# Chunked attention, then an ELU feed-forward network: exchanging 32x32 blocks of the turned probabilities by ScalarE copies in place of four transfers

## The chip, the core and the metric

The kernel runs on one core of a Trainium2 chip. The metric is the device time of the whole program in microseconds (us); less is better. "Before" is the kernel as it stood, "after" the changed one. The engines are named as the profile names them: PE (TensorE), PEld (its weight loads), DVE (VectorE), ACT (ScalarE), POOL (GpSimd), and SP (SyncE), which here issues every transfer.

## The reference

Softmax attention inside chunks of 64 tokens, then a feed-forward network on the 4608 rows of 512 features that it gives. q, k and v are 8 x 8 x 576 x 64 (batch, heads, tokens, head size), all in float32.

```
scores = q_c @ k_c.T / sqrt(64)            # per batch, head and chunk of 64 tokens
a      = exp(scores - max) / (sum + 1e-9)
x      = (a @ v_c)                         # back to 4608 x 512
h      = x @ w_in                          # 512 -> 2048
out    = elu(h) @ w_out                    # 2048 -> 512
```

## The kernel before

**The work.** The 4608 tokens are 9 blocks of 512 (`NB`), each of 4 tiles of 128 tokens (`NTT`); a tile holds two chunks of 64 tokens. The feed-forward part needs products in full float32, which are made from three products of a high and a low part (`three`, L434: `a_hi b_hi + a_hi b_lo + a_lo b_hi`). Blocks 0 to 2 do it plainly: for each of 16 slices `f` of the hidden features, 12 matmuls make `h` (`hidden`), ACT does relu and exp (L468, L469), DVE combines them to the elu (L471), ACT casts the high part (L476), DVE or POOL makes the low part (L479), and 12 matmuls add the slice to the output (`second_products`). The later blocks are taken in pairs as one 2 x 2 block product with seven products in place of eight (Strassen's scheme): one pair by code written out by hand (`Pair`, L725, then `KEPT`), the last two pairs of blocks from a planner (`Plan`, L820; there the exp is taken head by head, L1515).

**The attention of a tile** runs inside the feed-forward work of an earlier block, a step at a time. For tiles 8 to 35 (class `Later`) the steps are: load q and k (`load_qk`), transpose them on DVE in blocks of 32 x 32 (`turn`, L351), 32 score matmuls (`score`, L248), subtract the maximum (L361, L362), exp on ACT (L367), the sums on DVE (L372 to L374), then `turn_a`: multiply by the inverse sums (L380), transpose the probabilities on DVE (`turn_out`, L388) into `turned`, copy that to `unturned` on ACT (`copy_turned`, L393) and exchange blocks (`swap_turned`, L399). DVE's transpose turns each 32 x 32 block where it stands, so for a 64 x 64 chunk the two off-diagonal blocks still lie in each other's group of 32 partitions. `swap_turned` puts them right with four transfers of 32 x 256 floats (32 KB each): two chunks (`c`) times two blocks (`e`). Last come 32 matmuls with v (`times_v`, L256), which read `turned`, and a copy of the result (`keep_x`, L420).

**What sets the order.** Every engine carries out its instructions in the order in which the program gives them. In the third block that is a string for each `f` (`EVEN`, `ODD`, `THIRD_BLOCK`): `H` is `hidden(f)`, each `e` the next step of the elu, `P` the 12 output matmuls; `h` is `turn_a`, `q` and `k` the transposes, `s` the scores, `v` and `x` the product with v and its copy, `l` and `V` loads, `w` a step that prepares sums of w_out on POOL, ACT and DVE (L576 to L597). A tile takes two slices: `h` at the end of the odd slice or the start of the even one, `q` and `k` in the even one, `s` and `v` in the next odd one. In the pairs the items are `p1` to `p7` (a product of 6 matmuls), `c` (ACT copies it out, L758), `d` (DVE adds it up, L762), `1` to `4` (elu steps), `Q` (3 output matmuls) and the attention's letters. `SUMS_AT` says behind which items a `w` step goes. In the planner each job has engines with costs and keys that it reads and writes; a list scheduler gives each engine the ready job that is due first, where due times come from PE's sequence. The order that comes out is fixed when the program is built.

**Transfers** all go through SP's queue. A transfer is issued when SP reaches it, and each issue waits on one of eight transfer semaphores in turn, that is for the transfer eight places ahead of it; `swap_turned` waits besides for ACT's copy.

Of the kernel before, what the change touches and what calls it, by code (L numbers as in the profile page):

```python
# [20 lines left out]
def kernel(  # L21
# [19 lines left out]
    nc = tc.nc  # L41

    B, H, S, D = q.shape
# [4 lines left out]
    P = 128  # L48
    C = 64
# [6 lines left out]
    Q = 32  # L56
    PLAIN = 3
    NS = (NB - PLAIN) // 2
    NG = NF // 2
# [19 lines left out]
    turned, unturned = [const.tile([P, 2, H, Q], F32, name=name) for name in ("turned", "unturned")]  # L79
# [29 lines left out]
    def in_order(w):  # L109

        return w.rearrange("p (c b d) -> p b c d", b=4, d=Q)
# [218 lines left out]
    class Later:  # L330
# [42 lines left out]
            nc.vector.tensor_scalar_add(z_ps, z_ps, 1e-9)  # L373
            nc.vector.reciprocal(self.z, z_ps)  # L374

        def turn_a(self):

            nc.vector.tensor_tensor(  # L380
                out=self.scores, in0=self.scores, in1=self.z.broadcast_to([P, 2, NK, C]),
                op=ALU.mult)
            self.turn_out()
            self.copy_turned()
            self.swap_turned()
# [9 lines left out]
        def swap_turned(self):  # L395
            for c in range(2):
                for e in range(2):
                    to, of = [slice(c * C + i * Q, c * C + (i + 1) * Q) for i in (e, 1 - e)]
                    nc.sync.dma_start(out=turned[to, 1 - e], in_=unturned[of, e])  # L399

        def times_v(self):
            self.x_ps = banks[0][:, :, NK * C:].rearrange("p c (h t) -> p c h t", h=NK)
# [562 lines left out]
    def dma(n: int, took: float):  # L965
        return 540 * n, 540 * (n - 1) + 2000 + took, took

    class Tokens:
# [3 lines left out]
            self.now, self.following, self.after, self.done = now, following, None, set()  # L972

        def step(self, item: str):
            on = self.now if item in "mEzhvx" else self.following
            item = {"M": "m", "F": "E"}.get(item, item)
            if item == "l":
                if on and on.n + 1 < NB * NTT and not self.after:
                    self.after = Later(on.n + 1)
                    self.after.load_qk()  # L980
                return
            if not on or (on.n, item) in self.done:
                return
            self.done.add((on.n, item))
            {"m": on.less_max, "E": on.exp, "z": on.sums, "h": on.turn_a,
             "v": on.times_v, "x": on.keep, "q": lambda: on.turn(0), "k": lambda: on.turn(1),
             "s": on.score, "V": on.load_v}[item]()
            if item == "x":
                self.now, self.following, self.after = self.following, self.after, None

    def warm(n: int):
# [35 lines left out]

    EVEN, ODD = "l H e q e k e e P", "H s v e x V m E e e z h e P"  # L1030
    THIRD_BLOCK = {
# [16 lines left out]
    }  # L1048
    FIRST_PAIR = (
# [1 line left out]
        "3 3"  # L1051
    )
    SECOND_PAIR = (
        "p1 c1 5 5 h Q 4 p2 d1 4 Q q k p6 c2 1 Q Q 1 p5 1 1 Q l p7 c3 d2 Q Q 2 p4 c4 2 Q 3 p3 d3 "
        "3 3 3 s v x V"
    )
    PAIR = (
        "m p1 c1 4 E Q 4 z p2 d1 Q p6 c2 h 1 Q Q 1 p5 1 q k 1 Q l p7 c3 d2 Q Q 2 p4 c4 2 Q 3 p3 d3 "
        "3 3 3 s v x V"
    )  # L1060
    KEPT = (
# [16 lines left out]
    )  # L1078
    SUMS_AT = ("p1", "p2", "c2", "d2", "p4", "p3")

    ctx.enter_context(tc.manual_schedule(engines={
        mybir.EngineType.PE, mybir.EngineType.Activation, mybir.EngineType.DVE,
# [7 lines left out]
    with (  # L1090
# [19 lines left out]
        for item in START.split():  # L1110
            kind, n = item[0], item[1:]
# [61 lines left out]
    kept_st, unstored, banks, later, t3_place = [], [], [], {}, []  # L1173

    run, f, early_tiles = (0, o_tiles(), None), -1, {}
    for item in FIRST_BLOCK.split():
# [3 lines left out]
        elif item == "e":  # L1180
            g, acted = next(act), acted + 1
# [30 lines left out]
    for f in range(NF):  # L1212
        tt, st = divmod(f, 4)
        n = 2 * NTT + tt + 1
# [9 lines left out]
        for item in (LAST if f == NF - 1 else (LATER if tt else SECOND_BLOCK)[st]).split():  # L1224
            if item == "H":
                act, acted = elu(hidden(f)), 0
            elif item == "e":
                g, acted = next(act), acted + 1
# [21 lines left out]
    n = PLAIN * NTT  # L1250
# [61 lines left out]
    for f in range(NF):  # L1312
        for item in THIRD_BLOCK.get(f, ODD if f % 2 else EVEN).split():
            if item == "H":
                h = hidden(f)
                act, acted = elu(h, nc.gpsimd if 1 < f < NF - 1 else nc.vector), 0
            elif item == "e":
                g, acted = next(act), acted + 1
# [39 lines left out]
    for g in range(NG):  # L1358
        before, pair = pair, Pair(g)
        for item in ((FIRST_PAIR, SECOND_PAIR)[g] if g < 2 else PAIR).split():  # L1360
            if item[0] == "p":
                pair.product(int(item[1]))
            elif item[0] == "c":
                pair.keep(int(item[1]))
            elif item[0] == "d":
                pair.add(int(item[1]))
            elif item in "45":
                if before:
                    next(before.parts["3" if item == "5" else item], None)
            elif item in "123":  # L1370
                next(pair.parts[item])
            else:
                do(item)
            if item in SUMS_AT[4 if g == 0 else 0:4 if g == NG // 2 else 6] and g <= NG // 2:
                do("w")
    preparing, halves_kept, o_last = True, iter(range(NF)), o_tiles()
    run = n0 + TB, o_last, b_half_place
# [23 lines left out]
    plan = Plan()  # L1401
# [80 lines left out]
    def add_softmax(t: float, n: int, begun: bool = False):  # L1482
        mx = {}

        def in_bank(at: int = 0):
            at += NK * C
            return later[n].bank[:, :, at:at + NK].rearrange("p j (h e) -> p j h e", e=1)

        def maximum():
            mx[0] = in_bank(NK)  # L1490
            nc.vector.tensor_reduce(out=mx[0], in_=later[n].scores, axis=AX.X, op=ALU.max)

        def less():
            nc.vector.tensor_tensor(
                out=later[n].scores, in0=later[n].scores,
                in1=mx[0].broadcast_to([P, 2, NK, C]), op=ALU.subtract)

        def bias():
            mx[1] = sm.tile([P, 2, NK, 1], F32, name="mx")
            nc.vector.tensor_scalar_mul(mx[1], mx[0], -SCALE)  # L1500

        def normal():
            nc.vector.tensor_tensor(
                out=later[n].scores, in0=later[n].scores,
                in1=later[n].z.broadcast_to([P, 2, NK, C]), op=ALU.mult)

        plan.add(t + 1.0, "DVE", DVE_OP, maximum, ["psa"], [("mx", n), "xps"])
        if BY_HEADS and not begun:
            plan.add(t + 1.3, "DVE", (150, 172), bias, [], [("mx", n)])

            def exp_by_head():
                later[n].z = sm.tile([P, 2, NK, 1], F32, name="z")
                for j in range(2):
                    for h in range(NK):
                        nc.scalar.activation(  # L1515
                            out=later[n].scores[:, j, h, :], in_=later[n].scores[:, j, h, :],
                            func=AF.Exp, scale=SCALE, bias=mx[1][:, j, h, :],
                            accum_out=later[n].z[:, j, h, :])

                nc.scalar.activation(  # L1520
                    out=in_bank(), in_=later[n].z, func=AF.Copy, scale=1.0, bias=1e-9)

            def inverse():
                nc.vector.reciprocal(later[n].z, in_bank())
            plan.add(t + 2.0, "ACT", (2100, 2300), exp_by_head, [("mx", n)], ["psa"])
            plan.add(t + 2.5, "DVE", (190, 207), inverse, [], ["psa"])
        else:
            plan.add(t + 1.5, "DVE", DVE_OP, less, [], ["psa"])
            plan.add(t + 2.0, "ACT", ACT_PSUM, lambda: later[n].exp(), [], ["psa"])
            plan.add(t + 2.5, "DVE", (1000, 1110), lambda: later[n].sums(), [], ["psa"])  # L1530
        plan.add(t + 3.2, "DVE", DVE_OP, normal, [], ["psa"])
        plan.add(t + 3.7, "DVE", (630, 716), lambda: later[n].turn_out(), ["psa"], ["turned"])
        plan.add(t + 4.2, "ACT", ACT_OP, lambda: later[n].copy_turned(), ["turned"], ["unturned"])
        plan.add(t + 4.7, "SP", dma(4, 420), lambda: later[n].swap_turned(), ["unturned"], ["turned"])

    def add_turns(t: float, n: int):
        for i, to in enumerate(("qT", "kT")):
# [216 lines left out]
    for when, (job, f, tt, hi, lo) in zip([T0 - 1 + .05 * i for i in range(4)] + [T0 - .5 + .05 * i for i in range(4)],  # L1754
# [10 lines left out]
        if last:  # L1765
            place = g_first[:, 3, tt]
            e = "DVE" if tt % 2 else "ACT"
# [3 lines left out]
                             out=place.rearrange("p (b c d) -> p b c d", b=4, d=Q),  # L1771
                             in_=in_order(o_last[tt])),
# [3 lines left out]
                         out=out[n0 + TB + tt * P:n0 + TB + (tt + 1) * P, :], in_=place),  # L1776
# [59 lines left out]
```

## Time and profile before

| | |
|---|---|
| three timed runs | 839.7, 840.29 (median), 842.94 us |
| the profiled execution | 841.87 us, of which the span of the core's instructions is 840.1 us |
| PE busy in the span | 812.3 us (97%), 5853 matmuls |
| DVE, ACT, POOL busy | 620.0 us (74%), 525.0 us (62%), 172.8 us (21%) |
| transfers | 191.38 MB, mean 228 GB/s; 112 of them are `turned<-unturned` |
| mean granted PE clock | 0.991 of full speed |

The changed code runs in these stretches of the span, by the profile's own times: the third block from about 222 to 326 us, the pairs written by hand to 463, `KEPT` to 513, the first planned pair of blocks to about 700 us. Behind that no attention is left.

In a row of a list of groups stand line, engine and operation, out<-in by the program's names, sizes and count, and behind the bar the busy time in us, the mean of one in ns, and the engine's idle time just before with what ended most of it. In a row of the waits stand the waiting engine with its tile and line, what it waited for, and the total in us, the count and the longest. In a row of the timeline stand start in us, duration in us, engine, line and operation, and in brackets the idle time before it. PEclk is the clock granted to PE as a share of full speed.

### The profile page before, as it was taken

The numbers are of one execution on the slowest core, as the hardware profiler recorded it, in microseconds if no ns is written. First come the engines' busy times: TensorE is split into PE (matmuls) and PEld (weight loads), VectorE is DVE, ScalarE is ACT, GpSimd is POOL, SyncE is SP. The second block draws the span as 40 slices with busy tenths as digits, with TensorE's granted clock in tenths as the row PEclk, the third lists the DMA queues.
The fourth block names the chain that finished last, engine by engine and source line by source line (L and its number), as shares of the span: only waits on it lengthen the run. The fifth ranks groups of instructions, "written<-read, shape, count | busy, mean of one in ns | idle before, by whom it ended". The sixth has DMA issues, their size and how long they took to land.

```text
span 840.1 us, 15832 instructions
## 1 busy us (share of the span) xinstructions
PE 812.3 (97%) x5853; PEld 661.7 (79%) x5853; DVE 620.0 (74%) x908; ACT 525.0 (62%) x990; POOL 172.8 (21%) x147
## 2 busy tenths in 40 slices
PE   7899999999999989989999999999999999999996
PEld 6788888888778868868778888777888878888885
DVE  5999997666865748776756777867789956557954
ACT  5999876445544535755556544888967737776451
POOL 0000014365433411554211351000020000000101
PEclk9999999999999989999999999999999999999999
DMA  9974855889878986689997888998766585555654
GB/s 246 257 248 167 260 167 162 258 258 270 241 207 236 253 225 175 197 233 256 292 272 206 260 228 267 314 276 260 236 209 215 183 246 204 197 188 192 225 193 133
DMA packets 188653, 191.38 MB, mean 228 GB/s; under 512 B 82592, under 2 KB 157856, under 8 KB 188576
## 3 DMA queue, kind: packets, MB, share of 16 engines
q1 hardware_dynamic: 188576, 190.37, 75.7%
q8 instruction: 46, 0.75, 0.4%
q14 instruction: 31, 0.25, 0.1%
HBM read 143.65 MB, written 42.99 MB: 222 GB/s over the span
## 4 chain that ended last, share of the span: by engine, by line
PE 74%; DMA 12%; DVE 5%; SPq 4%; ACT 3%; issue 1%; DVEq 0%; ACTq 0%
PE o L434 41%; PE h L434 28%; DMA ring<-a_dram 2%; DMA turned<-unturned 2%; PE ps_a L256 2%; PE ps_a L248 2%; SPq L206 1%; DMA kept<-in_q_dram 1%; DMA v_sb<-in_v_dram 1%; DMA a_dram<-wi_hi 1%; DMA w_dram<-kept 1%; DMA st<-in_moe_w_out_dram 1%; DVE kept L542 1%; DMA w_dram<-g_kept 1%; SPq L227 1%
## 5 line engine op out<-in xcount | busy, mean ns | idle before, releaser
L434 PE MATMUL o<-wo_hi,ghi 128*128 128x512 f32 x272 | 108.7, 400 | 0.0
L434 PE MATMUL o<-wo_hi,glo 128*128 128x512 f32 x272 | 107.0, 394 | 0.2 <-DVE glo L479 0.2
L434 PE MATMUL o<-wo_lo,ghi 128*128 128x512 f32 x272 | 107.0, 393 | 0.0
L434 PE MATMUL h<-xhi,wi_hi 128*128 128x512 f32 x228 | 83.9, 396 | 0.0
L434 PE MATMUL h<-xlo,wi_hi 128*128 128x512 f32 x228 | 82.4, 390 | 0.5 <-DMA wi_hi<-a_dram 0.5
L434 PE MATMUL h<-xhi,wi_lo 128*128 128x512 f32 x180 | 70.2, 390 | 0.0
L434 PEld LDWEIGHTS o<-wo_hi,glo 128*128 128x128 f32 x272 | 51.6, 190 | 12.0 <-DVE glo L479 1.1
L434 PEld LDWEIGHTS o<-wo_hi,ghi 128*128 128x128 f32 x272 | 51.7, 190 | 11.4
L434 PEld LDWEIGHTS o<-wo_lo,ghi 128*128 128x128 f32 x272 | 51.7, 190 | 10.4
L510 POOL TENSOR_TENSOR kept<-wi_hi,wi_lo 128x512 f32<-128x512 f32 x16 | 24.8, 1566 | 156.1 <-DMA kept<-in_k_dram 116.4
L471 DVE SCALAR_TENSOR_TENSOR e<-e,h 128x512 f32<-128x512 f32 x48 | 32.8, 683 | 25.6 <-ACT e L469 25.6
L434 PE MATMUL o<-split,ring 128*128 128x512 f32 x216 | 50.9, 390 | 0.0
L434 PEld LDWEIGHTS h<-xhi,wi_hi 128*128 128x128 f32 x228 | 42.6, 188 | 9.7 <-ACT kept L758 0.6
L434 PEld LDWEIGHTS h<-xlo,wi_hi 128*128 128x128 f32 x228 | 42.7, 188 | 9.3 <-issue 0.9
L434 PEld LDWEIGHTS o<-split,ring 128*128 128x128 f32 x216 | 40.5, 188 | 8.4
L393 ACT COPY unturned<-turned 128x512 f32<-128x512 f32 x28 | 17.4, 620 | 45.4 <-DVE turned L388 45.4
L468 ACT ACTIVATE e<-h 128x512 f32<-128x512 f32 x48 | 28.8, 599 | 26.8 <-PE h L434 24.1
L476 ACT CAST ghi<-e 128x512 fp32r<-128x512 f32 x48 | 29.8, 621 | 19.5 <-DVE e L471 19.4
L434 PE MATMUL h<-split,ring 128*128 128x512 f32 x168 | 40.3, 391 | 0.0
L1441 ACT ACTIVATE e<-e 128x512 f32<-128x512 f32 x64 | 39.4, 630 | 1.1
L434 PEld LDWEIGHTS h<-xhi,wi_lo 128*128 128x128 f32 x180 | 33.8, 188 | 7.1
L361 DVE TENSOR_REDUCE mx<-ps_a 128x8 f32<-128x512 f32 x21 | 14.4, 688 | 32.0 <-ACT xf L420 31.4
(215 smaller groups left out, 2030.1 us busy)
## 6 DMA issues: line engine op xcount, KB each, us to landing
ring<-a_dram SPq DMA_DIRECT2D x56, 512.0 KB, 4.6
ring<-w_dram SPq DMA_DIRECT2D x56, 512.0 KB, 3.2
wi_hi<-a_dram SPq DMA_DIRECT2D x56, 256.0 KB, 5.9
kept<-in_q_dram SPq DMA_DIRECT2D x100, 128.0 KB, 3.0
kept<-in_k_dram SPq DMA_DIRECT2D x100, 128.0 KB, 3.7
wo_lo<-lo_dram SPq DMA_DIRECT2D x20, 512.0 KB, 6.2
v_sb<-in_v_dram SPq DMA_DIRECT2D x32, 256.0 KB, 5.1
st<-in_moe_w_in_dram SPq DMA_DIRECT2D x16, 512.0 KB, 4.3
```

Of the source, the lines that this page charges most:

```text
L206: nc.sync.dma_start(out=dst[p0:p0 + n], in_=src[b, :, s0:s0 + n, :].rearrange("h s d -> s h d"))
L227: nc.sync.dma_start(out=qk[p0:p0 + n // U, w0:w0 + NK * U * D].rearrange("p (h w) -> p h w", h=NK), in_=src[b, j::2, s0:s0 + n, :].rearran ...
L248: nc.tensor.matmul(scores[halves[c], j, hp, :], lhsT=qT[halves[j], hp, halves[c]], rhs=kT[halves[j], hp, halves[c]], start=True, stop=True,)
L256: nc.tensor.matmul(x_ps[halves[j], c, hp, :], lhsT=v_sb[halves[c], 2 * hp + j, :], rhs=aT[halves[c], :, j * NK + hp], start=True, stop=True,)
L361: nc.vector.tensor_reduce(out=mx, in_=self.scores, axis=AX.X, op=ALU.max)
L393: nc.scalar.copy(out=unturned, in_=turned)
L434: nc.tensor.matmul(ps, lhsT=a, rhs=b, start=start, stop=stop, skip_group_check=onto)
L468: nc.scalar.activation(out=e, in_=h, func=AF.Relu, scale=-1.0)
L471: nc.vector.scalar_tensor_tensor(out=e, in0=e, scalar=-1.0, in1=h, op0=ALU.add, op1=ALU.max)
L476: nc.scalar.copy(out=ghi, in_=e)
L510: nc.gpsimd.tensor_tensor(out=out, in0=a, in1=b, op=op)
L1441: nc.scalar.activation(out=units[u], in_=units[u], func=AF.Exp, scale=-1.0)
```

## The change

From the third block on, for 24 of the 28 tiles, `swap_turned` with its four transfers is not called; four ACT copies of 32 partitions x 256 floats, from one group of partitions to the other, write the same blocks. They come in two halves, one for each chunk (`swap_next`). In the third block both halves (`y y`) stand directly behind `H` of the even slice, and so ahead of that slice's relu and exp. In the pairs they stand behind `c3` and `c4`. In the planner each half is an ACT job of its own. `SUMS_AT` is moved so that one `w` step of the first pair falls in the second. The tiles of the second block keep the four transfers.

```diff
+        def turn_and_copy(self):
+            self.normalize()
+            self.turn_out()
+            self.copy_turned()
+            self.chunks = iter(range(2))
+
+        def swap_next(self):
+            c = next(self.chunks, None)
+            if c is not None:
+                for e in range(2):
+                    to, of = [slice(c * C + i * Q, c * C + (i + 1) * Q) for i in (e, 1 - e)]
+                    nc.scalar.copy(out=turned[to, 1 - e], in_=unturned[of, e])
...
-            {"m": on.less_max, "E": on.exp, "z": on.sums, "h": on.turn_a,
+            {"m": on.less_max, "E": on.exp, "z": on.sums, "h": on.turn_and_copy,
...
-    EVEN, ODD = "l H e q e k e e P", "H s v e x V m E e e z h e P"
+    EVEN, ODD = "l H y y e q e k e e P", "H s v e x V m E e e z h e P"
...
-        "m p1 c1 4 E Q 4 z p2 d1 Q p6 c2 h 1 Q Q 1 p5 1 q k 1 Q l p7 c3 d2 Q Q 2 p4 c4 2 Q 3 p3 d3 "
+        "m p1 c1 4 E Q 4 z p2 d1 Q p6 c2 h 1 Q Q 1 p5 1 q k 1 Q l p7 c3 y d2 Q Q 2 p4 c4 2 y Q 3 p3 d3 "
...
-        plan.add(t + 4.7, "SP", dma(4, 420), lambda: later[n].swap_turned(), ["unturned"], ["turned"])
+        for c in range(2):
+            plan.add(t + 4.7 + .1 * c, "ACT", (650, 850), swap(c), ["unturned"], ["turned", ("half", c)])
```

PE's order is the same in both kernels, instruction for instruction. What moves is shown at three places.

ACT's order in the third block, at the tile whose `h` is followed by a `w` step that casts `io`. First as before: `unturned<-turned` is `copy_turned`, `e<-h` and `e<-e` are relu and exp of the even slice.

```order
L393 COPY unturned<-turned 128x512
L588 CAST io<-io 128x1024
L468 ACTIVATE e<-h 128x512
L469 ACTIVATE e<-e 128x512
L476 CAST ghi<-e 128x512
```

The same place in the changed kernel:

```order
L393 COPY unturned<-turned 128x512
L601 CAST io<-io 128x1024
L412 COPY turned<-unturned 32x256 x4
L481 ACTIVATE e<-h 128x512
L482 ACTIVATE e<-e 128x512
```

The four copies stand between the attention's copy and the relu and exp of the slice; nothing else has moved there.

ACT's order in a pair of the hand-written part, from the copy of product 3 (`kept<-h`) to the elu of the second hidden slice (`e<-spare`), before:

```order
L758 COPY kept<-h 128x512
L708 ACTIVATE e<-g_kept 128x512
L709 ACTIVATE e<-e 128x512
L758 COPY spare<-h 128x512
L708 ACTIVATE e<-spare 128x512
```

And in the changed kernel:

```order
L771 COPY kept<-h 128x512
L412 COPY turned<-unturned 32x256 x2
L721 ACTIVATE e<-g_kept 128x512
L722 ACTIVATE e<-e 128x512
L771 COPY spare<-h 128x512
L412 COPY turned<-unturned 32x256 x2
L721 ACTIVATE e<-spare 128x512
```

Two copies stand ahead of each of the two elus.

SP's order in the third block, from a load of v on, before; `kept` is the place of the next q and k:

```order
L206 DMA v_sb<-in_v_dram 128x8x64
L399 DMA turned<-unturned 32x256 x4
L227 DMA kept<-in_q_dram 32x4x256 x4
L227 DMA kept<-in_k_dram 32x4x256 x4
L597 DMA w_dram<-io 128x4x256 x2
```

And in the changed kernel:

```order
L206 DMA v_sb<-in_v_dram 128x8x64
L227 DMA kept<-in_q_dram 32x4x256 x4
L227 DMA kept<-in_k_dram 32x4x256 x4
L610 DMA w_dram<-io 128x4x256 x2
L675 DMA wo_lo<-lo_dram 128x1024
```

The loads of q and k follow the load of v directly, and what stands behind them comes four issues sooner.

More of the change, by code (lines that the diff above doesn't have):

```diff
@@ L374, in sums, with normalize @@
             nc.vector.reciprocal(self.z, z_ps)
-        def turn_a(self):
+        def normalize(self):
             nc.vector.tensor_tensor(
@@ L382, in turn_a @@
                 op=ALU.mult)
+        def turn_a(self):
+            self.normalize()
             self.turn_out()
@@ L399, in swap_turned @@
                     nc.sync.dma_start(out=turned[to, 1 - e], in_=unturned[of, e])
+        def turn_and_copy(self):
+            self.normalize()
+            self.turn_out()
[7 more added lines that the diff above has]
+                    nc.scalar.copy(out=turned[to, 1 - e], in_=unturned[of, e])
         def times_v(self):
@@ L974, in step @@
         def step(self, item: str):
-            on = self.now if item in "mEzhvx" else self.following
+            on = self.now if item in "mEzhyvx" else self.following
             item = {"M": "m", "F": "E"}.get(item, item)
@@ L981, in step @@
                 return
+            if item == "y" and on:
+                on.swap_next()
+                return
             if not on or (on.n, item) in self.done:
@@ L1053 @@
     SECOND_PAIR = (
-        "p1 c1 5 5 h Q 4 p2 d1 4 Q q k p6 c2 1 Q Q 1 p5 1 1 Q l p7 c3 d2 Q Q 2 p4 c4 2 Q 3 p3 d3 "
+        "p1 c1 5 5 h Q 4 p2 d1 4 y Q q k p6 c2 y 1 Q Q 1 p5 1 1 Q l p7 c3 y d2 Q Q 2 p4 c4 2 y Q 3 p3 d3 "
         "3 3 3 s v x V"
@@ L1078 @@
     )
-    SUMS_AT = ("p1", "p2", "c2", "d2", "p4", "p3")
+    SUMS_AT = {0: ("p3",), 1: ("p1", "p2", "p6", "p5", "d2", "p4", "p3"),
+               4: ("p1", "p2", "c2", "d2"), 5: (), 6: (), 7: ()}
+    SUMS_AT[2] = SUMS_AT[3] = ("p1", "p2", "c2", "d2", "p4", "p3")
     ctx.enter_context(tc.manual_schedule(engines={
@@ L1373 @@
                 do(item)
-            if item in SUMS_AT[4 if g == 0 else 0:4 if g == NG // 2 else 6] and g <= NG // 2:
+            if item in SUMS_AT[g]:
                 do("w")
@@ L1500, in bias, with swap, run_ @@
             nc.vector.tensor_scalar_mul(mx[1], mx[0], -SCALE)
+        def swap(c: int):
+            def run_():
+                if not c:
+                    later[n].chunks = iter(range(2))
+                later[n].swap_next()
+            return run_
         def normal():
```

24 rows, old and new, of tables (KEPT, THIRD_BLOCK) are left out of this document.

## The prediction, written before the changed kernel was run

> **What bounds the kernel now.** I read the page's busy times, then the waits of PE by stretches, then the granted clock behind the longest waits, then the timeline of ACT, DVE and PE around each exchange. The first two lines of the page:
>
> ```profile
> PE 812.3 (97%) x5853; PEld 661.7 (79%) x5853; DVE 620.0 (74%) x908; ACT 525.0 (62%) x990; POOL 172.8 (21%) x147
> PEclk9999999999999989999999999999999999999999
> ```
>
> PE is busy for 97% of the span, so the change can only win what PE loses in waits and at a lower clock. It can lose what ACT's extra work makes PE wait. The waits of PE in four stretches (243 to 247, 305 to 313, 371 to 378, 380 to 513 us), and then in three behind 513 us:
>
> ```profile
> PE ps_a L256 <- DMA turned<-unturned: 1.1, 2, 0.9
> PE ps_a L256 <- DMA kept<-in_q_dram: 3.6, 1, 3.6
> PE ps_a L256 <- DMA turned<-unturned: 2.1, 2, 1.7
> PE ps_a L256 <- DMA turned<-unturned: 0.8, 2, 0.5
> PE o L434 <- DVE g_kept L1444: 1.0, 1, 1.0
> PE h L434 <- DMA ring<-a_dram: 0.6, 1, 0.6
> PE h L434 <- DMA ring<-a_dram: 1.2, 1, 1.2
> ```
>
> L256 is the product with v, which reads `turned` and v. The 3.6 us are put down to a load of q, which L256 doesn't read. The timeline of SP and PE shows what it is:
>
> ```profile
> 301.09 0.42 SPq L206 DMA_DIRECT2D v_sb<-in_v_dram  x1
> 301.61 3.64 SPq L399 DMA_DIRECT2D turned<-unturned  x4
> 306.44 0.69 PE L248 MATMUL ps_a<-k_turned,qT 64*64 64x64 f32 x32
> 310.70 1.52 PE L256 MATMUL ps_a<-turned,v_sb 64*64 64x64 f32 x32 [3.57 <-DMA kept<-in_q_dram]
> DMA to landing us min/median/max: 6.2/7.3/8.7
> ```
>
> The four transfers took 3.64 us to issue, and the landing row of this line and stretch gives 6.2 to 8.7 us each; the product began at 310.70, when the last was in. So the exchange cost PE 1.1 + 3.6 + 2.1 + 0.8 = 7.6 us of waits. The stretches behind the two long waits, and around the 1.1 us one, in the view of windows (PEclk stands behind POOL's count):
>
> ```profile
> 310.70:317.00 6.30, 6.30 (x45) 5.07 (x46) 3.83 (x8) 1.73 (x3) 1.29 (x1) 0.56 0.75 212
> 377.40:381.40 4.00, 4.00 (x18) 3.13 (x11) 1.39 (x2) 1.70 (x3) 2.81 (x5) 0.57 1.05 247
> 242.00:246.00 4.00, 2.87 (x70) 2.12 (x69) 1.47 (x1) 1.58 (x4) 4.00 (x3) 1.00 0.66 167
> ```
>
> After the long waits the clock fell to 0.56 and 0.57 for a while: 6.3 x 0.44 = 2.8 us and 4.0 x 0.43 = 1.7 us more, 4.5 us together. Around the wait of 1.1 us it stayed at 1.00. A rule stands against the second of these terms. The Trainium skill (TensorE: Matmul & The Clock Gate, Part 1, What's actually happening) has the clock drop after at least one idle window of about 3.4 us; a wait of 2.1 us would then be free of it, the clock term would be 2.8, and the sum 6.9 us won in place of 8.6. The trace disagrees (0.57 behind a wait of 2.1 us), so I keep 4.5.
>
> **What the change removes.** 24 tiles lose four transfers each, 96 in all; 16 of 112 stay, in the second block. All four stretches above lie behind the second block, so 7.6 + 4.5 = 12.1 us of PE's time lose their cause. SP loses 96 issues, and 96 places among the eight outstanding transfers. That can only bring other loads forward; the rows for what it could win are the two waits for `ring`, 0.6 and 1.2 us, but `ring` is also held by PE's own use of its places. I count nothing, and 1.8 us as the bound.
>
> **What the change adds.** Four ACT copies of 256 floats a partition for each tile. No such copy is in the trace; the nearest rows are a cast of the same length on all partitions, and the copy of 512:
>
> ```profile
> L684 ACT CAST wo_lo<-xf 128x256 fp32r<-128x256 f32 x4 | 1.6, 407 | 2.3 <-DVE xf L693 2.3
> L393 ACT COPY unturned<-turned 128x512 f32<-128x512 f32 x28 | 17.4, 620 | 45.4 <-DVE turned L388 45.4
> L1515 ACT ACTIVATION_READ_ACCUMULATOR ps_a<-ps_a,mx 128x1 f32 x56 | 10.8, 193 | 0.0
> ```
>
> One copy then takes about 0.41 us. Back to back, operations of ACT overlap: a copy from 288.41 to 289.03 was followed by a cast at 288.94 (rows below), so 0.09 us less each, and four take 4 x 0.32 = 1.3 us. The bounds are 4 x 0.19 = 0.8 (an operation that moves next to nothing) and 4 x 0.62 = 2.5 (the copy of 512). I take 1.3, since the cast has the same length. ACT gets 24 x 1.3 = 31 us more and goes from 525 to about 556 of 840 us, so it stays below PE; what counts is where the copies stand.
>
> *Third block, eight tiles.* The copies stand ahead of the slice's relu and exp. DVE's elu step waits for these, and `k_turned` is queued behind it on DVE; the scores wait for `k_turned`. So each `k_turned` comes 1.3 us later. Three tiles have less than that to spare. The timeline of DVE and PE at the first, second, fourth, sixth and seventh tile, the sixth with ACT's rows, and of ACT at the eighth:
>
> ```profile
> 228.99 1.11 DVE L351 STREAM_TRANSPOSE k_turned<-kept 128x512 f32<-128x512 f32 x1
> 230.44 0.69 PE L248 MATMUL ps_a<-k_turned,qT 64*64 64x64 f32 x32
> ...
> 240.54 1.11 DVE L351 STREAM_TRANSPOSE k_turned<-kept 128x512 f32<-128x512 f32 x1
> 243.03 0.69 PE L248 MATMUL ps_a<-k_turned,qT 64*64 64x64 f32 x32
> ...
> 268.22 1.09 DVE L351 STREAM_TRANSPOSE k_turned<-kept 128x512 f32<-128x512 f32 x1
> 269.46 0.69 PE L248 MATMUL ps_a<-k_turned,qT 64*64 64x64 f32 x32 [0.28 <-DVE k_turned L351]
> ...
> 288.41 0.62 ACT L393 COPY unturned<-turned 128x512 f32<-128x512 f32 x1 [2.14 <-DVE turned L388]
> 288.94 1.05 ACT L588 CAST kept<-kept 128x1024 fp32r<-128x1024 f32 x1
> 292.99 1.10 DVE L351 STREAM_TRANSPOSE k_turned<-kept 128x512 f32<-128x512 f32 x1
> 294.24 0.69 PE L248 MATMUL ps_a<-k_turned,qT 64*64 64x64 f32 x32
> ...
> 303.37 1.10 DVE L351 STREAM_TRANSPOSE k_turned<-kept 128x512 f32<-128x512 f32 x1
> ...
> 317.68 0.62 ACT L393 COPY unturned<-turned 128x512 f32<-128x512 f32 x1 [2.14 <-DVE turned L388]
> 319.89 0.60 ACT L468 ACTIVATE e<-h 128x512 f32<-128x512 f32 x1 [1.59 <-PE h L434]
> ```
>
> First tile: `k_turned` ends at 230.10, would end at 231.4, scores due at 230.44: 1.0 us of wait. Second: 241.65 becomes 242.95, due at 243.03: none. Fourth: 269.31, and PE waited for it already: 1.3 in full. Sixth: 294.09 becomes 295.39, due at 294.24: 1.2. The seventh ended at 304.47 with scores at 306.44 (quoted above), 2.0 us to spare, and the third and fifth are like it. In the eighth ACT waited 1.59 us for PE's `h` behind its copy, and the four copies fit in there. These lose nothing. Together 3.5 us. Each is near the wait of 1.1 us that left the clock at 1.00, so I add nothing for the clock; if one dropped it, that would cost 1.7 us. With 0.8 for the four copies the sum is 1.9 us, with 2.5 it is 9.7, since then every tile but the eighth shows some.
>
> *Hand-written pairs, seven tiles; KEPT, two.* Behind `c3` ACT waits for DVE's sum before the next elu, and behind `c4` the elu's DVE step is queued behind the sum of product 3:
>
> ```profile
> 391.37 0.63 ACT L708 ACTIVATE e<-g_kept 128x512 f32<-128x512 f32 x1 [1.19 <-DVE g_kept L762]
> 393.23 0.63 ACT L708 ACTIVATE e<-spare 128x512 f32<-128x512 f32 x1
> 393.90 0.63 ACT L709 ACTIVATE e<-e 128x512 f32<-128x512 f32 x1
> 395.51 0.68 DVE L712 SCALAR_TENSOR_TENSOR e<-e,spare 128x512 f32<-128x512 f32 x1
> 463.00:513.00 50.00, 50.00 (x286) 41.22 (x279) 34.44 (x37) 22.22 (x35) 21.53 (x14) 1.00 0.81 249
> ```
>
> The first two copies (0.65 us) lie in the 1.19 us of waiting; behind the last exp, which ended at 394.53, DVE took its step at 395.51, 0.98 us later, which hides the other two. In `KEPT` ACT is busy 22.2 of 50 us. I take zero; without this cover it would be 0.65 a pair, 4.6 us.
>
> *Planned part, seven tiles.* Here ACT is fullest:
>
> ```profile
> 525.00:546.00 21.00, 20.00 (x147) 16.10 (x146) 17.63 (x29) 17.68 (x44) 1.31 (x1) 1.00 1.01 314
> 588.00:609.00 21.00, 21.00 (x153) 17.24 (x152) 16.73 (x27) 18.98 (x52) 1.29 (x1) 1.00 0.78 237
> ```
>
> A tile's 1.3 us fit into the 2 to 3 us that ACT has left in 21, and at 588 to 609, with ACT at 18.98, PE lost nothing: the planner gives the splits to ACT ahead of their product. I take zero, with 7 x 1.3 = 9.1 as the bound.
>
> **The sum.** Profiled execution: 841.87 (span 840.1 and 1.8 around it) - 7.6 - 4.5 + 3.5 = 833.3 us, so 8.6 us less. The median of the runs shown is 840.29, 1.6 below the profiled one; 840.29 - 8.6 = 831.7 for the median.
>
> **The rivals.**
> *ACT becomes the bound (slower).* Each tile's copies stand in front of work that PE needs. It decides when more than 12.1 / 1.3 = 9 of the 24 tiles show their 1.3 us in full. Likeliest are the eight of the third block and the seven planned ones: 15 x 1.3 = 19.5, less 12.1, gives +7.4: 847.7. For it: ACT at 18.98 of 21 us. Against: only three of eight tiles are short in the third block. 0.06.
> *The wait goes to the next late transfer.* The two long waits came in a crowded queue; if the next load behind is as late, 5.7 us and the clock's 4.5 stay. Then 1.9 are won and 3.5 lost: 841.9. Against: the matmul that stood still waited for the last of the four itself, and the scores' q and k were there. 0.09.
> *The transfers were hidden already.* A transfer issued early and waited for late costs PE nothing; then only the 3.5 us of copies are left: 843.8. Against are the seven waits quoted; the product comes 5 us behind the issue, while a landing took up to 8.7. 0.04. The Trainium skill (DMA: Bandwidth & Descriptors, Rules for kernel authors) advises just this, issue early and wait late, so that the fixed cost overlaps; the trace agrees for the tiles that show no wait, not for these.
> *Nothing new shows.* `k_turned` finds room, since less on SP brings loads and other work forward: 840.29 - 12.1 = 828.2; with the waits for `ring` and the 1.0 us behind 513 gone too, 12.1 + 2.8: 825.4. 0.20.
>
> **The numbers.** The forecast keeps 0.61. Its own range is 830 to 838 (waits of 1.9 to 9.7 us together in the third block). The range 825 to 838 takes in the forecast and the last rival, 0.81. What can be told from no change is 0.5%, 4.2 us: under 836.1 is faster, over 844.5 slower. Faster: 0.61 less 0.05 for the dear copies, and 0.20: 0.76. Slower: 0.06. Between: 0.09 + 0.04 + 0.05 = 0.18.
>
> **What would show it.** Right: no wait of L256 for a transfer, clock at 1.00 through 300 to 320 and 370 to 385 us, copies `turned<-unturned` near 0.41 us, three waits of L248 for `k_turned` near 1 us in the third block, `KEPT` still without a wait. Wrong: copies over 0.6 us, more than three such waits, PE waiting for ACT or DVE between 513 and 660 us, or waits for `wi_hi` or `ring` of several us that weren't there.

## The result, and the profile after

| | before | changed |
|---|---|---|
| median of 4 runs, us | 840.19 (839.7 to 842.94) | 847.04 (846.27 to 848.11) |
| ratio | | 1.0076, 95% interval 1.005 to 1.0101 |
| profiled execution, us | 841.87 | 848.11 |
| its span, us | 840.1 | 846.3 |

The change makes the kernel slower by 0.8%, where 1% faster was forecast. The changed kernel's page, busy times and the granted clock by slices:

```profile
PE 809.6 (96%) x5853; PEld 657.8 (78%) x5853; DVE 619.6 (73%) x908; ACT 561.8 (66%) x1086; POOL 171.9 (20%) x147
PEclk9999999999999999999999999999999999999999
```

ACT has 37 us more, 96 copies of 0.404 us; PE is busy for no longer than before (809.6 and 812.3), in a span that is 6.2 us longer: it waits more. The waits of PE in four stretches (220 to 330, 345 to 463, 513 to 665, 665 to 835 us):

```profile
PE ps_a L248 <- DVE k_turned L351: 7.2, 6, 2.1
PE h L447 <- DMA wi_hi<-a_dram: 2.7, 2, 1.5
PE o L447 <- DMA ring<-a_dram: 1.7, 1, 1.7
PE o L447 <- ACT kept L1435: 1.1, 1, 1.1
PE o L447 <- ACT spare L1435: 1.1, 1, 1.1
PE h L447 <- DMA ring<-a_dram: 3.9, 1, 3.9
```

Every wait of L256 for the exchange is gone, as forecast. In its place there are six waits for `k_turned`, two for ACT in the planned part, and at 687 us a long one for `ring`, far behind the last exchange.

Where the time goes is read best from marks that PE passes in both runs, since its order is the same. The marks are the first product with v behind the second block, then the last of the third block, of the pairs and of `KEPT`, the last of all, and the last matmul. In the changed kernel, from the timeline of PE:

```profile
218.12 0.65 PE L256 MATMUL ps_a<-turned,v_sb 64*64 64x64 f32 x32
327.93 0.68 PE L256 MATMUL ps_a<-turned,v_sb 64*64 64x64 f32 x32
461.77 0.73 PE L256 MATMUL ps_a<-turned,v_sb 64*64 64x64 f32 x32
522.07 0.65 PE L256 MATMUL ps_a<-turned,v_sb 64*64 64x64 f32 x32
661.76 0.69 PE L256 MATMUL ps_a<-turned,v_sb 64*64 64x64 f32 x32
839.23 0.39 PE L447 MATMUL o<-ghi,ring 128*128 128x512 f32 x1
```

Before, they stand at 215.56, 325.68, 462.46, 522.22, 659.23 and 832.97. The differences give what each stage lost or won against the profiled execution of before (us, + is longer). The row "changed, again" is a second profile of the changed kernel, the rows behind it are the experiments below; "planned" reaches to the last product with v, "rest" from there to the last matmul.

| profiled run | start | third block | pairs | KEPT | planned | rest | sum |
|---|---|---|---|---|---|---|---|
| forecast | 0 | -4.0 | -4.6 | 0 | 0 | 0 | -8.6 |
| changed | +2.6 | -0.3 | -2.9 | +0.5 | +2.7 | +3.7 | +6.3 |
| changed, again | +0.1 | +1.9 | -5.1 | +0.9 | +2.7 | +3.7 | +4.3 |
| third block's copies late | +1.9 | -6.4 | -5.1 | +0.8 | +2.6 | +3.9 | -2.3 |
| planned part by transfers | +1.0 | +0.8 | -3.4 | +0.8 | +0.6 | 0.0 | -0.3 |
| both | +2.3 | -7.0 | -5.0 | +0.8 | +0.6 | -0.4 | -8.6 |
| pairs and KEPT by transfers | +0.5 | +1.7 | +1.6 | 0.0 | +2.4 | +5.3 | +11.5 |
| copies, not in the plan | +1.6 | +0.2 | -4.3 | +0.6 | +3.2 | +4.5 | +5.7 |
| transfers, in the new plan | +0.2 | +0.7 | -4.2 | +0.6 | +1.7 | +0.8 | -0.3 |
| ring ahead of the stores | +2.2 | +0.5 | -5.0 | +0.8 | +2.8 | -0.4 | +0.8 |
| that and the late copies | +1.9 | -6.9 | -4.6 | +0.5 | +6.3 | -0.3 | -3.1 |
| third block flat | +2.5 | -4.6 | -4.6 | +0.5 | +2.4 | +3.6 | -0.2 |
| third block by transfers | +1.0 | -1.7 | -5.8 | +0.8 | +2.4 | +5.3 | +2.0 |

The first column lies ahead of every changed instruction: 0.1 to 2.6 us by chance. So some 2 us of the first profile's 6.3 aren't the change's. The other columns are single profiles too: in seven profiles with the same copies in the third block that stage came out between -0.3 and +1.9, and it was -1.7 in one that had before's transfers back. A difference of 2 us or less in one stage is therefore not clear of chance.

### The profile page after: what moved, and what is told of

Read it like the earlier page. It is cut to its first block, busy times and chain, and to the rows that moved or that the text cites. A ratio compares the mean times of both kernels' runs of the same rounds, so it can differ in the third digit from the quotient of the medians.

```text
span 846.3 us, 15707 instructions
## 1 busy us (share of the span) xinstructions
PE 809.6 (96%) x5853; PEld 657.8 (78%) x5853; DVE 619.6 (73%) x908; ACT 561.8 (66%) x1086; POOL 171.9 (20%) x147
## 4 chain that ended last, share of the span: by engine, by line
PE 64%; ACT 11%; DMA 9%; DVE 8%; SPq 4%; issue 3%; POOL 0%; DVEq 0%; ACTq 0%; POOLq 0%
PE o L447 34%; PE h L447 25%; DMA ring<-a_dram 3%; DMA wi_hi<-a_dram 2%; DMA kept<-in_k_dram 2%; PE ps_a L248 2%; SPq L206 1%; ACT turned L412 1%; PE ps_a L256 1%; PE h L464 1%; ACT ps_a L1540 1%; DVE k_turned L351 1%; ACT e L1456 1%; ACT e L1459 1%; ACT e L482 1%
## 5 line engine op out<-in xcount | busy, mean ns | idle before, releaser
L412 ACT COPY turned<-unturned 32x256 f32<-32x256 f32 x96 | 38.8, 404 | 1.8
```

The source lines that it names most:

```text
L412: nc.scalar.copy(out=turned[to, 1 - e], in_=unturned[of, e])
```

## What the trace says, and the theories

The first tile of the third block in the changed kernel, ACT's timeline:

```profile
228.55 0.62 ACT L393 COPY unturned<-turned 128x512 f32<-128x512 f32 x1 [2.96 <-DVE turned L388]
229.20 1.65 ACT L412 COPY turned<-unturned 32x256 f32<-32x256 f32 x4
230.87 0.60 ACT L481 ACTIVATE e<-h 128x512 f32<-128x512 f32 x1
```

The four copies take 1.65 us, and the relu starts 2.32 us behind the start of the `unturned` copy. Without copies the next operation started 0.53 behind it (288.41 and 288.94 in the prediction). So a tile's copies move ACT by 1.79 us, not by 1.3: a copy starts when the one before it has ended, and so does the relu.

The end, in four rows of DVE, SP, SP and PE of the changed kernel:

```profile
682.01 0.67 DVE L1612 STREAM_TRANSPOSE g_kept<-kept 128x512 f32<-128x512 f32 x1
682.11 4.42 SPq L1620 DMA_DIRECT2D out_dram<-g_kept  x8
686.63 0.98 SPq L1295 DMA_DIRECT2D ring<-a_dram  x2
691.08 4.12 PE L447 MATMUL h<-wo_lo,ring 128*128 128x512 f32 x11 [3.92 <-DMA ring<-a_dram]
```

And the first and the last of these before:

```profile
676.54 0.66 DVE L1586 STREAM_TRANSPOSE g_kept<-kept 128x512 f32<-128x512 f32 x1
685.85 3.00 PE L434 MATMUL h<-wo_lo,ring 128*128 128x512 f32 x12 [1.21 <-DMA ring<-a_dram]
```

This is the fourth of VectorE's transposes into `g_kept` there. It ends at 682.68 against 677.20, 5.5 us later, while PE was 2.5 us later at the last product with v. SyncE issues the eight stores of what these transposes write, which takes 4.4 us, and only then the two loads of `ring` that PE needs. SyncE's order was the same before, but there PE waited only 1.2 us for these loads.

My theory (A) was that the place of the copies costs: in the third block ahead of relu and exp, in the planned part on an ACT that is full, with the wait for `ring` as its late end. The rivals: what was lost in the third block is given back there anyway (B), the waits for `ring` are chance (C), or SyncE, rid of its transfers, runs ahead and crowds the queue (D).

## The experiments

**The third block's copies behind relu and exp.** In `EVEN` and the eight even rows of `THIRD_BLOCK`:

```
-    EVEN, ODD = "l H y y e q e k e e P", "H s v e x V m E e e z h e P"
+    EVEN, ODD = "l H e y y q e k e e P", "H s v e x V m E e e z h e P"
```

> Third block: the four copies go behind the slice's relu and exp instead of ahead of them; nothing else moves. Theory A (the copies' place in ScalarE's queue holds up k_turned, and the scores): the six waits for k_turned of together 9.3 us fall to about 0.3, the third block ends about 5 us earlier against the run before (2.3 us late becomes about 3 early), and the time is 840 to 842 us. Rival B (what was lost in the third block was given back there anyway, since the waits for the exchange behind it get shorter): the time stays at 846 to 848.

839.03 us (6 runs), ratio to before 0.9949 (0.9913 to 0.9985). PE's wait in the third block:

```profile
PE ps_a L248 <- DVE k_turned L351: 1.5, 3, 0.9
```

The waits fell from 7.2 to 1.5 us (not to 0.3: 0.27 and 0.30 at the fourth and the sixth tile, and the eighth kept its 0.95), and the stage won 6.4 us in place of 0.3. A holds, B falls: what the place cost was not given back.

**The planned part by four transfers, as before.**

```
-        for c in range(2):
-            plan.add(t + 4.7 + .1 * c, "ACT", (650, 850), swap(c), ["unturned"], ["turned", ("half", c)])
+        plan.add(t + 4.7, "SP", dma(4, 420), lambda: later[n].swap_turned(), ["unturned"], ["turned"])
```

> Planned part alone goes back to four transfers a tile, and with them to the plan of before; third block, pairs and KEPT copy. Theory A (the planned part on ScalarE is full, and the copies push its splits, the sums and at the end the stores back): the waits behind 513 us for kept and spare (1.1 each) go, the wait for ring at 687 us falls from 3.9 to about 1.2, 6 to 7 us are won: 840 to 842 us. Rival C (the wait for ring is a matter of when its transfers happen to land, and comes in any plan): no more than 2 us, 845 to 847.

842.06 us (10 runs, 838.27 to 846.89), ratio 0.999 (0.9963 to 1.0017). The waits for `kept` and `spare` are gone, and behind 665 us PE waits for `ring`:

```profile
PE h L447 <- DMA ring<-a_dram: 1.2, 2, 1.0
```

By the table the stages behind 522 us lose 0.6 in place of 6.4. A's reading of the place holds, C falls, though against before the time shows no difference.

How copies on ACT make VectorE late shows in VectorE's waits for ACT's exp over the whole run, in the changed kernel and then before:

```profile
DVE g_kept L1462 <- ACT e L1459: 16.0, 11, 6.5
DVE g_more L1462 <- ACT e L1459: 7.7, 7, 2.5
DVE g_kept L1444 <- ACT e L1441: 5.0, 6, 2.5
DVE g_more L1444 <- ACT e L1441: 4.5, 8, 1.1
```

Between 513 and 677 us all of VectorE's waits for ACT's `e` come to 12.9 us in the changed kernel, 4.0 before, and 3.2 in this run.

**Pairs and KEPT by transfers, the rest copies.**

```
-                on.swap_next()
+                (20 <= on.n <= 28) or on.swap_next()
...
-            {"m": on.less_max, "E": on.exp, "z": on.sums, "h": on.turn_and_copy,
+            {"m": on.less_max, "E": on.exp, "z": on.sums, "h": on.turn_a if 20 <= on.n <= 28 else on.turn_and_copy,
```

> Hand-written pairs and KEPT alone go back to transfers; third block and planned part copy. Theory A: the waits of 1.9 and 1.6 us for wi_hi go, the waits of L256 for turned come back (2.1 and 0.8, and about 1.7 us of half clock): 847 to 849 us. Rival D (SyncE, rid of the transfers, runs ahead, and its loads crowd the queue; that is what costs time from the pairs on, the wait for ring included): 841 to 844.

853.33 us (4 runs), ratio 1.0101 (1.0071 to 1.013). Between 345 and 463 us:

```profile
PE ps_a L256 <- DMA turned<-unturned: 3.0, 6, 1.1
PE h L447 <- DMA wi_hi<-a_dram: 2.5, 3, 1.0
```

The waits for the exchange are back, and those for `wi_hi` didn't go, though A had said so. They are no mark of the copies: the second profile of the changed kernel has none. D is refuted: more transfers made it slower, by more than A said. The pairs lost 1.6 us in place of winning 2.9 to 5.8. Here the change is worth what was forecast.

**Six forms of the copy.** For its time alone, in the third block's tiles 1 to 8:

```
+    FORMS = {14: lambda a, b: (b, b), 15: lambda a, b: (b, b),
+             16: lambda a, b: (slice(0, P),) * 2, 17: lambda a, b: (slice(0, Q),) * 2,
+             18: lambda a, b: (slice(Q, 2 * Q), slice(0, Q)),
+             19: lambda a, b: (slice(C, P), slice(0, C))}
...
+                    to, of = FORMS.get(self.n, lambda a, b: (a, b))(to, of)
                     nc.scalar.copy(out=turned[to, 1 - e], in_=unturned[of, e])
```

> The third block's copies take six forms, four copies to a tile, for their duration alone: tiles 1 and 2 as they are (32 partitions, moved to the other group), 3 and 4 without the move, 5 on all 128 partitions without a move, 6 four on the first 32 partitions without a move, 7 four with the same move from partitions 0-31 to 32-63, 8 four from the lower to the upper 64. The exchange is then not done in tiles 3 to 8. Theory E (the move between partition groups keeps a copy from overlapping with the next): starts 0.41 us apart in tiles 1, 2, 7 and 8, 0.32 in 3 to 6. Rival F (it is the change of partitions from one copy to the next): 0.41 in 1 to 4, 0.32 in 5 to 8. Rival G (any copy of 256 a partition goes at this rate): 0.41 everywhere. Time as the changed kernel's, 846 to 848.

846.38 us (one run). ACT's timeline at tiles 1, 3, 5, 6, 7 and 8 (start, length of the four, and the start of what follows at tiles 5 and 7):

```profile
228.41 1.65 ACT L413 COPY turned<-unturned 32x256 f32<-32x256 f32 x4
...
253.94 1.66 ACT L413 COPY turned<-unturned 32x256 f32<-32x256 f32 x4
...
281.04 1.33 ACT L413 COPY turned<-unturned 128x256 f32<-128x256 f32 x4
282.27 0.59 ACT L482 ACTIVATE e<-h 128x512 f32<-128x512 f32 x1
...
295.09 1.32 ACT L413 COPY turned<-unturned 32x256 f32<-32x256 f32 x4
...
307.95 1.33 ACT L413 COPY turned<-unturned 32x256 f32<-32x256 f32 x4
309.30 0.60 ACT L482 ACTIVATE e<-h 128x512 f32<-128x512 f32 x1
...
320.26 1.32 ACT L413 COPY turned<-unturned 64x256 f32<-64x256 f32 x4
```

Rival F, for the copies: not the move between groups (tile 7 moves and takes 1.33), nor the number of partitions (tile 6 has 32), but whether the next copy starts at other partitions than the last (tile 3 moves nothing, alternates, and takes 1.66). The operation behind is held too if its partitions start elsewhere: the relu started 1.35 us behind the first copy at tiles 7 and 8, whose copies write from partition 32 and 64 on, and 1.23 and 1.22 at tiles 5 and 6, whose copies write from partition 0 on, as the relu does. The Trainium skill (VectorE: DVE Perf Modes, Two Vector instructions with no wait between them) has a rule of this kind for VectorE, as a model: an instruction whose input or output starts in another group of 32 partitions than the last one's in the same memory is held until all earlier VectorE instructions have finished. These rows show the like on ScalarE. The exchange's four copies all start elsewhere, so each pays.

**Late copies and transfers in the planned part together** (the edits of the first two).

> Two edits together: the third block's copies behind relu and exp, and the planned part by transfers in the plan of before. Theory A (the losses are the place of the third block's copies and what the planned part's copies do there): the gains add up, 839.0 less the 6 us that the planned part lost in that run behind 513 us: 832 to 835. Rival H (with PE some 9 us earlier, the planned part's transfers and loads come too late in their turn): 837 to 840.

832.92 us (5 runs, 831.69 to 833.86), ratio 0.9881 (0.9861 to 0.9902). PE's waits for `k_turned` in the third block are those of the run with late copies alone, 1.5 us in three tiles.

The two gains add up, as A said, and H falls. This kernel beats both. It keeps the copies of the third block, the pairs and `KEPT`, and the changed kernel's `SUMS_AT`, which was not tried alone.

**The planner isn't told of the copies.**

```
-            plan.add(t + 4.7 + .1 * c, "ACT", (650, 850), swap(c), ["unturned"], ["turned", ("half", c)])
+            plan.add(t + 4.7 + .1 * c, "ACT", (1, 1), swap(c), ["unturned"], ["turned", ("half", c)])
```

> As the changed kernel, but the planner is told that a chunk's copies take 1 ns of ScalarE: the copies stay, 1.66 us a tile, and the order of the other engines is near that of before. Theory A1 (in the planned part it is the copies' own time on a full ScalarE that costs): the waits for kept and spare stay or grow, PE is again 3 us or more later at 660 us than at 513, and the wait for ring at 687 us is 3 us or more; 846 to 849. Rival A2 (it is the planner's new order of the sums, splits and stores): the wait for ring falls to about 1.2 and the waits for ScalarE go; 841 to 843.

848.39 us (4 runs), ratio 1.0071 (1.0043 to 1.0099). Behind 665 us:

```profile
PE h L447 <- DMA ring<-a_dram: 3.6, 1, 3.6
```

**Transfers, in the changed kernel's plan.** In the planned part alone, `swap` keeps its ACT time in the plan and issues two transfers. `send_next` is `swap_next` with this line in place of the copy:

```
+        def send_next(self):
...
+                    nc.sync.dma_start(out=turned[to, 1 - e], in_=unturned[of, e])
...
-                later[n].swap_next()
+                later[n].send_next()
```

> The converse: the changed kernel's plan, with ScalarE's time for the copies set aside in it, but at their places the four transfers are issued, and no copy is made in the planned part. Theory A1: 841 to 843, the wait for ring about 1.2. Rival A2 (the new order is what costs): 846 to 848, with the wait for ring near 4 and the stores ahead of it late.

843.15 us (10 runs), ratio 1.0001 (0.9983 to 1.0019). Behind 665 us:

```profile
PE h L454 <- DMA ring<-a_dram: 2.1, 2, 1.4
```

With the copies, in an order that lies between the old one and the new, the time is lost; with the new order and no copies most of it isn't (1.7 us in "planned" and 0.8 in "rest", against 0.6 and 0.0 in the old plan). VectorE says it more plainly. Its fourth transpose into `g_kept` ends 20.9 us behind the start of the last product with v in the changed kernel and 21.5 without the planner's knowledge of the copies, but 18.0 before, 17.8 with transfers in the old plan and 17.7 with transfers in the new one. So A1: it is the copies' own time on ACT. The 1.9 us by which the new plan's two stages lie above the old plan's may be the plan's, but no more than chance moves a stage.

**The changed kernel again.** No edit.

> The changed kernel once more, beside the others on the same chip. If what PE lost in its first 215 us (1.6 to 2.6 us, in code that the change doesn't touch) was chance, this run's delay there lies elsewhere between 0 and 2 us, as in the runs so far (0.15 to 1.9); the six waits for k_turned (7.2 us) and the wait for ring at 687 us (about 4) come again. 846 to 848; the ratio to before 1.003 to 1.008, since before spread from 838 to 848 on the last chip.

847.59 us (4 runs), ratio 1.0057 (1.0036 to 1.0079), on a chip where before took 842.38 (15 runs). The start lay 0.1 us off this time. The six waits for `k_turned` (7.3 us) and the one for `ring` at the end (3.7) came again. The waits for `wi_hi` did not: PE has none between 345 and 463 us, and the pairs win 5.1 us in place of 2.9. So that wait of the first profile was chance.

**Loads of ring ahead of the stores.** Two `send`s of `add_out` are held back until two loads of `ring` are issued; only SyncE's order changes:

```
         nc.sync.dma_start(out=slot.bitcast(F32), in_=of)
+        if held_back:
+            held_back[0] -= 1
+            if not held_back[0]:
+                for go in held_back[1:]:
+                    go()
+                held_back.clear()
...
         def send():
+            if s == 1 and h:
+                held_back or held_back.append(2)
+                held_back.append(send_now)
+            else:
+                send_now()
```

> The changed kernel with one step of SyncE's order turned round: the two loads of ring that stand behind eight stores of g_kept (682.1 to 686.6 us) are issued ahead of them; no other engine's order changes. Theory J (the copies make VectorE late, its g_kept makes the stores late, and the stores keep the loads of ring waiting in SyncE's queue): the wait of 3.7 to 3.9 us for ring at 687 us falls below 1, and 3 to 4.5 us are won: 843 to 844. Rival K (the place of ring or the transfer itself is late, not SyncE's queue): the wait stays, 846 to 848.

842.63 us (10 runs, 840.42 to 846.34), ratio 1.0006 (0.9983 to 1.0029). SP's timeline:

```profile
672.26 8.48 SPq L1295 DMA_DIRECT2D ring<-a_dram  x4
680.79 7.46 SPq L1635 DMA_DIRECT2D out_dram<-g_kept  x12
```

And the product that had waited 3.9 us:

```profile
685.67 2.88 PE L447 MATMUL h<-wo_lo,ring 128*128 128x512 f32 x12
```

It starts without a wait, though VectorE's fourth `g_kept` ends 20.9 us behind the last product with v, as in the changed kernel. The stage won 0.4 us in place of losing 3.7. J holds: the loss there was the place of two loads behind eight stores in SyncE's queue, brought out by a late VectorE. The time came out a little below the 843 to 844 that J gave.

**That order and the late copies.**

> That step together with the third block's copies behind relu and exp; the planned part still copies. Theory J: 839.0 less 3 to 4.5 us: 834.5 to 836. Then the kernel with transfers in the planned part (832.9) stays ahead by what ScalarE's copies cost between 513 and 660 us, about 2. Rival K: 839.

835.94 us (10 runs, 833.4 to 839.39), ratio 0.9929 (0.9904 to 0.9954). As J said. By the ratios to before, the kernel with transfers in the planned part stays 0.5% ahead, some 4 us where about 2 were expected. In this profile, of one of the longer of the ten runs (838.79 us), "planned" lost 6.3 us: PE waited 3.2 us for `ring` at 531 us, where the longest such wait in the other experiments' profiles was 0.9 to 2.1 us, and the clock lay at 0.70 for the 8 us from 532 us on. No run tells why.

**The copies at the price that I had forecast.** For its time alone, `FORMS` sends all eight tiles' copies from partitions 0-31 to 0-31, so that the exchange isn't done there:

```
+    FORMS = {n: lambda a, b: (slice(0, Q),) * 2 for n in range(12, 20)}
```

> The third block's four copies all go from partitions 0-31 to partitions 0-31, so that they overlap and take about 1.33 us a tile in place of 1.66, at the same place ahead of relu and exp. The exchange is left out in these tiles. It shows what the price that I had forecast would have done. Theory M (place and price both count; each tile that waits for k_turned waits 0.45 us less): six or five waits of together 4.5 to 5.5 us in place of 7.3. Rival N (with the price as forecast, the forecast's three waits of 3.5 us come): 3 to 4 us, in three tiles.

841.72 us (one run). PE's wait in the third block:

```profile
PE ps_a L248 <- DVE k_turned L351: 4.5, 4, 1.5
```

Its rows at the first, fourth, sixth and eighth tile, and the clock for 4 us behind the two longest:

```profile
233.47 0.69 PE L248 MATMUL ps_a<-k_turned,qT 64*64 64x64 f32 x32 [0.96 <-DVE k_turned L351]
272.15 0.69 PE L248 MATMUL ps_a<-k_turned,qT 64*64 64x64 f32 x32 [1.51 <-DVE k_turned L351]
298.13 0.69 PE L248 MATMUL ps_a<-k_turned,qT 64*64 64x64 f32 x32 [1.51 <-DVE k_turned L351]
323.06 0.69 PE L248 MATMUL ps_a<-k_turned,qT 64*64 64x64 f32 x32 [0.47 <-DVE k_turned L351]
```

```profile
272.10:276.10 4.00, 3.95 (x77) 3.41 (x77) 1.98 (x3) 1.18 (x3) 2.50 (x3) 1.00 1.06 248
298.10:302.10 4.00, 3.97 (x77) 3.44 (x78) 3.06 (x4) 1.68 (x4) 0.00 (x0) 1.00 1.14 236
```

The three tiles are those of the forecast, at 0.96, 1.51 and 1.51 us where it had 1.0, 1.3 on top of 0.28, and 1.2; the eighth's 0.47 it didn't have. The clock stayed at 1.00. The stage won 4.6 us; 4.0 had been forecast. So M and N are each half right, and the place with the forecast price would still have won: it was the price that turned this stage.

**The third block by transfers, the rest copies** (the edit for the pairs with `on.n <= 19`).

> Third block alone goes back to transfers, the rest copies. If the forecast's first term was right, the waits of L256 for turned come back in the third block (1.1 and 3.6 us, with the clock near 0.56 behind the long one, 2.8 us more) and the waits for k_turned go: PE is about as late at 325 us as at 230. Rival (the wait of 3.6 us belonged to how the queue of before happened to stand): no wait over 1 us, and PE 5 us or more earlier at 325 than with the copies. Time 845 to 848, or 841 by the rival.

843.85 us (one run), somewhat under the 845 to 848 expected. PE's waits in the third block, and the clock at 310 to 318 us:

```profile
PE ps_a L256 <- DMA turned<-unturned: 4.5, 3, 3.3
PE ps_a L248 <- DVE k_turned L351: 0.6, 2, 0.3
```

```profile
310.00:318.00 8.00, 6.93 (x52) 5.77 (x53) 4.50 (x9) 1.73 (x3) 1.29 (x1) 0.79 0.76 213
```

The long wait comes again at the same tile, now put down to `turned` itself, with the low clock behind it. Between this kernel and the one with late copies the stage differs by 4.7 us: what removing the transfers is worth there, less what the late copies add to the waits for `k_turned` (1.5 us against 0.6 here). The stage itself lies 1.7 us below before's, with the same transfers, by chance as far as is known.

## Why the forecast was wrong, point by point

Two steps of the sum failed, by about as much each: the price of a tile's copies, which cost the third block 3.7 to 5.9 us against the forecast, and the zero for the planned part, which was 6.4 us.

- *What the transfers cost* (12.1 us): the mechanism was right. The waits of L256 are gone, the pairs won 2.9 to 5.8 us where 4.6 was forecast, and the third block won 6.4 to 7.0 once the copies stood elsewhere. The size was near: between kernels with transfers and with copies, the pairs differ by 4.5 to 7.4 us (4.6 forecast) and the third block, its copies late, by 4.7 (7.5 forecast).
- *A tile's copies take 1.3 us*: **the first step that failed.** It took the overlap of 0.09 us from operations that start at the same partitions. It was 1.79 us. By the forecast's own working that gives 1.45 for the first tile, 0.41 for the second, 1.79 for the fourth and 1.64 for the sixth, 5.3 us together in place of 3.5. Measured were 1.42, 0.51, 2.02 and 2.12 at these, 0.17 at the third and 0.94 at the eighth: 7.2 in six tiles. The eighth's isn't the place's doing, since it was 0.95 with the late copies too, and neither are some 0.3 us each at the fourth and the sixth, which were there with the late copies (0.27 and 0.30) and with transfers (0.27 and 0.28). Without these the waits come to 5.7 us in five tiles, near the 5.3. With the forecast price, in the run with flat copies, the stage won 4.6 us where 4.0 had been forecast.
- *No loss of clock behind these waits*: failed with it. The wait of 2.0 us at the fourth tile halved the clock for 4 us (1.7 us more), that of 2.1 at the sixth did not. The 2.1 us behind which the forecast read 0.57 were two waits, of 1.66 and 0.40 us, with 0.3 us of work between. PE's rows with their waits, and the windows behind them, in the changed kernel:

```profile
273.91 0.95 PE L248 MATMUL ps_a<-k_turned,qT 64*64 64x64 f32 x32 [2.02 <-DVE k_turned L351]
302.03 0.69 PE L248 MATMUL ps_a<-k_turned,qT 64*64 64x64 f32 x32 [2.12 <-DVE k_turned L351]
```

```profile
273.90:277.90 4.00, 3.99 (x70) 3.45 (x71) 1.49 (x3) 0.59 (x2) 2.43 (x2) 0.57 1.05 239
302.00:306.00 4.00, 3.97 (x77) 3.43 (x78) 3.05 (x4) 1.68 (x4) 0.00 (x0) 1.00 1.10 235
```

- *Pairs hide their copies*: right, as the stage's gain shows. `KEPT` lost 0.5 to 0.9 us wherever it copied and 0.0 in the one profile where it didn't. No row shows a wait there, and the cause stays open.
- *The planned part hides its copies* (zero, bound 9.1): **the second step that failed**, with 2.7 us up to the last product and 3.7 behind it, against 0.6 and 0.0 with transfers. ACT's free time per 21 us was the wrong measure. It said nothing of what comes late further on: ACT's exp and splits, VectorE's sums, then SyncE's stores, and behind them a load. That a relieved SyncE can only bring loads forward was wrong in the same way: the two loads of `ring` stood behind stores that waited for a late VectorE, and came later than before.
- *The rivals*: "ACT becomes the bound" gave the nearest time (847.7, at 0.06), in part by luck. Its places were half right: six of eight tiles in the third block, but in the planned part only two waits for ACT, of 1.1 us each; the large piece was a load behind the last exchange. "The wait goes to the next late transfer" did not come in the third block. In the pairs PE waited for `wi_hi`, by chance as the second profile shows, and in the planned part for `ring`.

Still open: why before itself ran from 837 to 848 us on the later chips, while the changed kernel stayed within 846.1 to 848.4; and what `SUMS_AT` is worth by itself.

## What to carry to other kernels

Price a new operation at the place where it will stand, with its neighbours: an overlap read from other shapes is not its own. Work that nobody waits for still belongs behind the work that somebody waits for; the same four copies two steps later turned a loss into a gain. And where an engine is said to have room, follow what it feeds to the next queue that runs in order, and look at what stands behind the late item there.

## What the runs showed of the hardware

- ScalarE: copies of 32x256 start 0.31 us apart if their partitions start where the last one's did, and 0.42 if not; each takes 0.40 either way.
- The clock: in seven profiles with the same copies (the changed kernel twice, and five of the experiments), PE waited 2.0 to 2.25 us at the fourth and at the sixth tile; in nine of these fourteen places the clock of the next 4 us fell to 0.57 to 0.64, in five it stayed at 1.00. Behind the waits of 1.4 to 1.5 us at the first tile of the same seven it stayed at 1.00. The second profile of the changed kernel, at both:

```profile
272.10:276.10 4.00, 4.00 (x71) 3.35 (x72) 2.03 (x4) 1.25 (x3) 2.41 (x2) 0.64 1.06 240
300.30:304.30 4.00, 4.00 (x70) 3.45 (x71) 2.53 (x4) 1.03 (x3) 0.00 (x0) 0.57 1.09 230
```

  The Trainium skill (TensorE: Matmul & The Clock Gate, Part 1, What's actually happening) lets the clock drop after at least one idle window of about 3.4 us, and has the window run free of the kernel. The trace disagrees with the length, as before; that the same wait costs or doesn't by chance fits a free-running window, which no run here shows by itself.
